# Two wide blocks a batch, near units of four blocks that may cross two batches, and softmax sums taken from a column of ones

## The chip, the cores and the metric

The kernel runs on one core of one Trainium2 chip. The metric is device microseconds of one execution; a kernel is judged by the median of several. A core has TensorE (PE in the profile; its weight loads are PEld), VectorE (DVE), ScalarE (ACT), GpSimd (POOL) and SyncE (SP, which here only issues DMAs). Every engine works through its own instructions in order and waits for others through semaphores.

## The reference

Block-sparse attention over 4 batches of 8 heads, 768 positions and 64 features, followed by a channel mix with a gate. Blocks are of 32 positions, 24 a batch.

```python
mask = np.abs(blk_i - blk_j) <= window            # window = 1
mask = mask | (blk_i == 0) | (blk_j == 0) | (blk_i == n_blocks - 1) | (blk_j == n_blocks - 1)
for qb in range(n_blocks):
    for kb in sampled_blocks[qb]:                 # three drawn blocks a row of blocks
        mask[qb * block:(qb + 1) * block, kb * block:(kb + 1) * block] = True
attn = softmax(where(mask, scale * q @ k.T, -1e9)) @ v
...
xk = mu_k * x + (1.0 - mu_k) * x_prev             # x is attn, heads side by side: 768 x 512
xr = mu_r * x + (1.0 - mu_r) * x_prev
k = np.maximum(xk @ w_k, 0.0)                     # 512 -> 1024
v = k * k @ w_v                                   # 1024 -> 512
out = sigmoid(xr @ w_r) * v
```

So query blocks 0 and 23 see every key, and each of the other 22 sees eight slots of 32 keys: the two end blocks, itself and its two neighbours, and three drawn blocks. A slot can repeat another one: a drawn block can be an end block, a neighbour or an earlier draw, and near the ends a neighbour is an end block. Such a repeat must count once.

## The kernel before

**Units.** A unit is four query blocks of one batch, 128 rows. Each batch has one wide unit, made of blocks 21, 22, 23 and 0 (`WIDE_BLOCKS`, line 32), and five near units of blocks 1 to 20. `UNITS` (line 202) starts with the wide units of batches 0, 1 and 2, then two near units of batch 0, then the wide unit of batch 3, then the other near units.

**A wide unit** (`wide_pair`, line 552) goes through four pairs of heads. For a pair, TensorE multiplies 128 query rows by 384 keys at a time (`sw`, line 563; two heads lie in the two halves of the contracted partitions), VectorE adds a mask and finds the extreme while it copies to `p` (`soft`, line 479), ScalarE takes exp and the sum with it (`exp`, line 489), TensorE transposes (`tw`, line 500), ScalarE copies the transposed tile (line 504), and TensorE multiplies by V, four blocks side by side in the array's columns (`o`, line 585). The keys lie in `k_ring`, which shares the memory tagged `k2` with the mixer's hidden values: the mixer's `k2` can't be taken before the last wide unit has let go of the ring.

**A near unit** is two groups of four heads (`near_group`, line 512). Each of the four blocks has its own tile of eight key slots (`KR`, five of them) and its own two tiles of V rows (`VR`, six): the three neighbours come by a plain load (line 468), the last block and the three drawn ones by a gather on POOL's queue (line 470). For a group there are 32 score matmuls in the profile (16 in the program, two passes each for f32) over 256 keys (`s`, line 524), then mask and extreme on VectorE, exp on ScalarE, two turns of four transposes (`t`, line 500) copied by VectorE (line 506), and 64 matmuls with V (`o`, line 546). Repeats are masked by -8e9 (`near_mask`).

**Finish** (line 593): reciprocal of the sums, the scaling, four transposes (`tx`, line 606) and the copy into `xt`, the transposed attention output of the batch. The wide units of batches 2 and 3 are finished long before their `xt` exists, so they go to a scratch tensor in HBM and come back later (`away`).

**The mixer** goes through three windows of 256 positions a batch, twelve in all. `split_x` (line 662) makes `xr` and `xk`, each as a pair of rounded high and low parts; every product is three matmuls. A window is two gates (`r`, line 713), four hidden pairs (`h`, line 731), squares on ScalarE and POOL, and two value products (`v`, line 760). Window 0 needs blocks 0 to 8 of its batch.

**Weights** arrive as float64 (10.5 MB) and are decoded by ScalarE, three VectorE operations (lines 365, 369, 373) and two POOL operations (lines 383, 387) for each of 20 tiles: 4 for `wr`, 8 for `wk`, 8 for `wv`.

**PSUM's eight banks**: two score tiles of two banks (`s`), one `o`, two for turns (`t`), one for the mixer (`m`).

**Order.** All operations are handed to a planner (`Plan`, line 83) with an estimated duration and a rank. `order` simulates the engines, picks among the operations that can start by rank, and so fixes the order in which each engine gets its instructions. The ranks come from tuned constants (line 844 and on); on the chip nothing but data waits and the order itself remain.

## Time and profile before

| what | value |
|---|---|
| median of 3 runs | 605.68 us (604.22 to 605.9) |
| profiled execution, span from first to last instruction | 616.1 us |
| PE busy in that span | 575.8 us (93%) |
| PEld, POOL, DVE, ACT busy | 465.5, 344.0, 303.8, 300.6 us |
| bytes moved by DMA | 114.18 MB, mean 185 GB/s |

The profiled execution has no time of its own beside its span; the span is 10.4 us (1.7%) longer than the median. Durations in the profile are of that execution, so a sum made of them stands against 616.1 us. Busy time of PE counts a matmul from its start to a modelled end, so some waiting inside a run of matmuls counts as busy.

### The profile page before, as it was taken

The page shows a single profiled execution, that of the slowest core. Times are in us where ns is not written, and L with a number is a line of the kernel's source. Part 1 is how long each engine was busy: PE and PEld are TensorE (multiplying, and loading weights), DVE is VectorE, ACT ScalarE, POOL GpSimd, SP SyncE. Part 2 cuts the span into 40 slices and gives each one's busy share as a digit, 9 for nine tenths or more (in the row PEclk, how much of TensorE's full clock was granted, in tenths as well). Part 3 has the DMA queues.
Part 4 walks back from the last instruction along what each step waited for, and adds up shares of the span by engine and source line. Part 5 has one row for each costly group of instructions (what it writes and reads, how often), then busy time and mean ns, then how long its engine had stood idle before and what let it go on. Part 6 is the DMA issues. An engine that isn't in the chain of part 4 may idle for free.

```text
span 616.1 us, 20666 instructions
## 1 busy us (share of the span) xinstructions
PE 575.8 (93%) x8172; PEld 465.5 (76%) x8172; DVE 303.8 (49%) x906; ACT 300.6 (49%) x712; POOL 344.0 (56%) x400
## 2 busy tenths in 40 slices
PE   8887878798899999999999989999999999999997
PEld 3564655587667878878788778778778788989897
DVE  6677768873864255264443452653632532423300
ACT  3675845583544545355535534635545454333341
POOL 1324344865777737657836835546467464664551
PEclk9999989999899999999999999999999999999999
DMA  8959659858786667766764774774666620000001
GB/s 310 399 157 379 231 168 335 282 164 286 219 261 217 188 193 212 210 181 202 227 200 164 232 227 146 233 229 147 224 188 182 201 75 1 36 18 18 17 18 35
DMA packets 88499, 114.18 MB, mean 185 GB/s; under 512 B 12626, under 2 KB 59219, under 8 KB 88403
## 3 DMA queue, kind: packets, MB, share of 16 engines
q1 hardware_dynamic: 81570, 91.79, 46.7%
q0 software_dynamic: 6400, 20.98, 10.7%
q8 instruction: 65, 1.06, 0.7%
q10 hardware_dynamic: 432, 0.10, 0.2%
q14 instruction: 32, 0.25, 0.1%
HBM read 106.01 MB, written 6.82 MB: 183 GB/s over the span
## 4 chain that ended last, share of the span: by engine, by line
PE 63%; DVE 10%; ACT 8%; issue 6%; POOL 5%; DMA 3%; another core or an unknown queue 2%; SPq 2%; ACTq 0%; DVEq 0%; POOLq 0%
PE v L760 17%; PE o L546 5%; PE h_1p L731 5%; PE h_3p L731 5%; PE r_0p L713 5%; PE t L500 5%; PE r_1p L713 4%; PE h_2p L731 4%; ACT p L489 4%; PE s L524 3%; PE h_0p L731 2%; PE tw L500 2%; PE sw L563 2%; PE o L585 2%
## 5 line engine op out<-in xcount | busy, mean ns | idle before, releaser
L760 PE MATMUL v<-wv,k 128*128 128x512 f32 (+1 forms) x600 | 139.4, 386 | 1.4 <-DVE z L768 1.4
L760 PEld LDWEIGHTS v<-wv,k 128*128 128x128 f32 x600 | 107.5, 188 | 26.5 <-DVE xr_2f L680 2.1
L489 ACT ACTIVATE p<-p,nm 128x256 f32<-128x256 f32 x160 | 79.4, 498 | 48.7 <-DVE nm L479 48.7
L470 POOL DMA_INDIRECT VR<-vt,lines x80 | 79.0, 988 | 33.1 <-PE o L546 16.0
L506 DVE COPY pt<-t 128x512 f32<-128x512 f32 x80 | 53.0, 686 | 81.5 <-PE t L500 74.6
L479 DVE CUSTOM_DVE_ANT_1 p<-s,near_mask 128x256 f32<-128x256 f32 x160 | 57.9, 418 | 30.4 <-remote 19.4
L689 POOL TENSOR_TENSOR xr<-xr_1f,xr 128x256 fp32r<-128x256 f32 x24 | 17.7, 740 | 72.0 <-ACT xr L687 71.9
L524 PE MATMUL s<-KR,q 64*32 64x256 f32 x1280 | 50.8, 381 | 1.0 <-PE tw L500 0.9
L500 PE MATMUL t<-ident,p 128*128 128x128 f32 x320 | 47.5, 283 | 3.8 <-ACT p L489 2.3
L546 PEld LDWEIGHTS o<-VR,pt 128*32 128x32 f32 x2560 | 37.9, 110 | 15.0 <-issue 8.8
L546 PE MATMUL o<-VR,pt 128*32 128x64 f32 x2560 | 44.7, 221 | 2.3 <-issue 1.4
L687 ACT CAST xr<-xr_1f 128x256 fp32r<-128x256 f32 x24 | 9.7, 405 | 72.9 <-PE r_0p L713 43.0
L731 PE MATMUL h_1p<-xk,wk 128*128 128x256 f32 x288 | 37.0, 283 | 8.2 <-ACT h_0k L744 4.6
L609 DVE TENSOR_TENSOR x<-o,R 128x512 f32<-128x512 f32 x24 | 16.6, 691 | 56.8 <-PE o L546 53.7
L500 PEld LDWEIGHTS t<-ident,p 128*128 128x128 f32 x320 | 36.9, 144 | 9.3 <-ACT p L489 6.4
L731 PEld LDWEIGHTS h_1p<-xk,wk 128*128 128x128 f32 x288 | 34.7, 188 | 10.3 <-ACT h_0k L744 5.5
L731 PEld LDWEIGHTS h_0p<-xk,wk 128*128 128x128 f32 x288 | 34.9, 188 | 3.6 <-issue 3.3
L713 PE MATMUL r_1p<-wr,xr 128*128 128x512 f32 x144 | 37.7, 411 | 0.0
L524 PEld LDWEIGHTS s<-KR,q 64*32 64x32 f32 x1280 | 27.1, 105 | 13.8 <-issue 3.8
L731 PE MATMUL h_3p<-xk,wk 128*128 128x256 f32 x288 | 36.8, 282 | 0.4 <-ACT h_2k L744 0.4
L731 PEld LDWEIGHTS h_2p<-xk,wk 128*128 128x128 f32 x288 | 34.6, 188 | 3.3 <-ACT k L745 3.3
L731 PE MATMUL h_0p<-xk,wk 128*128 128x256 f32 x288 | 36.9, 283 | 0.0
(115 smaller groups left out, 1043.7 us busy)
## 6 DMA issues: line engine op xcount, KB each, us to landing
VR<-vw SPq DMA_DIRECT2D x80, 256.0 KB
KR<-kd SPq DMA_DIRECT2D x80, 192.0 KB
KR<-kt SPq DMA_DIRECT2D x240, 64.0 KB
k_ring<-kq SPq DMA_DIRECT2D x16, 384.0 KB
VR<-vt SPq DMA_DIRECT2D x24, 256.0 KB
q<-qt SPq DMA_DIRECT2D x23, 256.0 KB
out<-z SPq DMA_DIRECT2D x23, 256.0 KB
early_w<-w_k SPq DMA_DIRECT2D x8, 512.0 KB
```

The lines of the kernel that those rows point to most:

```text
L470: plan.add(POOL, GATHER, at - LEAD_V + 0.01 * j, lambda w=w, n=n: nc.gpsimd.indirect_dma_start(VR[w].ap[:, 1, :], None, vt.rearrange("b n ...
L479: nc.vector.tensor_tensor_reduce(out=p.ap[:, cs].rearrange("p (a x) -> p a x", x=BLK), in0=view().rearrange("p (a x) -> p a x", x=BLK), in ...
L489: plan.add(ACT, 280 + 0.83 * (cs.stop - cs.start), rank, lambda: nc.scalar.activation(p.ap[:, cs], p.ap[:, cs], AF.Exp, bias=nm.ap[:, col ...
L500: nc.tensor.transpose(tp.ap[:, i, :], p.ap[:, cs], ident.ap)
L506: plan.add(DVE, 600, rank + 0.1, lambda: nc.vector.tensor_copy(out=pt.ap, in_=tp.ap), reads=[(tp,)], writes=[(pt,)])
L524: nc.tensor.matmul(s.ap[ROWS[j], row, a * 256 : (a + 1) * 256].rearrange("p (n x) -> p n x", x=BLK), q.ap[half, hp, ROWS[j]], KR[keys[j]]. ...
L546: nc.tensor.matmul(o.ap[ROWS[j], h * D : (h + 1) * D], pts[i // 2].ap[:, 2 * (i % 2) + g, ROWS[j]], VR[values[j]].ap[:, g, h * D : (h + 1) ...
L609: plan.add(DVE, 600, rank, lambda: nc.vector.tensor_tensor(out=x.ap.rearrange("p (h d) -> p h d", d=D), in0=o.ap.rearrange("p (h d) -> p h ...
L689: plan.add(POOL, 80 + 2.4 * MIX * tw, rank + O_MIX, lambda f=f, cs=cs: nc.gpsimd.tensor_tensor(out=dst.ap[:, 1, cs], in0=f.ap, in1=dst.ap[ ...
L713: nc.tensor.matmul(pr.ap[:, 0:512], xr.ap[:, a, c, :], wr.ap[:, w, c, :], start=(c == 0 and m == 0), stop=(c == CC - 1 and m == 2))
L731: nc.tensor.matmul(ph.ap[:, ff * TT : (ff + 1) * TT], wk.ap[:, w, c, f * P : (f + 1) * P], xk.ap[:, a, c, :], start=(c == 0 and m == 0), s ...
L760: nc.tensor.matmul(pv.ap[:, 0:width], k2.ap[:, a, f, i * P : (i + 1) * P], wv.ap[:, w, f, cs], start=(f == 0 and m == 0), stop=(f == FC - ...
```

## The change

**Units.** A wide unit is now two blocks, 0 and 23, which see all keys without a mask. The 22 near blocks of two batches make 44, that is eleven near units of exactly four blocks; the sixth is mixed (blocks 21 and 22 of the first batch, 1 and 2 of the second). In all there are 4 wide and 22 near units, ordered pair of batches by pair: wide, two near, wide, three near, mixed, five near. The scratch tensor in HBM is gone, and so is `k_ring`: wide keys lie in the same `KR` tiles as near keys, of which there are two, each for a whole unit.

**Wide.** With 64 query rows, two head pairs lie side by side in the array's columns: a score matmul is a 64x64 tile over 384 keys. VectorE finds the extremes of one score tile in one reduction. Half a unit (`wide_unit`, four heads) takes both score tiles.

**Near.** The keys of a unit are one run of six neighbouring blocks, two ends and twelve drawn blocks. A score matmul of 256 keys becomes one of 192 (three neighbours and three drawn) and one of 64 (the ends). There is no mask: repeats get V rows that are zero (row 3072 on of `vt`, through the gather's list), and V has a 65th column of ones, so the product with V gives the sum too, without the repeats. VectorE finds four extremes in one reduction over the 1024 scores; ScalarE takes exp straight from PSUM and no longer adds up. Turns are copied by ScalarE, except one in four from unit 6 on.

**Buffers.** Turns, finishes and mixer share two PSUM banks tagged `m`; `o` has two. `dif` goes from two buffers to one, `pt` from four to three. For unit 1 the drawn keys are loaded from ScalarE's queue.

**Planner.** It gets larger durations, a limit of eight DMAs in flight, and a model of PE's instruction supply (`code`, `feed`); release times and ranks are now lists, one for each unit, window and weight tile.

```diff
+QB = 4
+NEARS = NB - 2
+
+
+def near_units(pair):
+    b, c = 2 * pair, 2 * pair + 1
+    units = [[(b, n + j) for j in range(QB)] for n in range(1, NB - QB, QB)]
+    mixed = [(b, NB - 3), (b, NB - 2), (c, 1), (c, 2)]
+    return units, mixed, [[(c, n + j) for j in range(QB)] for n in range(3, NB - 1, QB)]
+
+
+ENDS, DRAWN = 2 * QB, 2 * QB + 2
+KEYS = DRAWN + QB * NRAND
+DV = D + 1
+HD = H * DV
...
-UNITS = [(0, 0), (1, 0), (2, 0), (0, 1), (0, 2), (3, 0)]
-UNITS += [(b, u) for b in range(B) for u in range(1, NC + 1) if (b, u) not in UNITS]
-
-AWAY = 2
...
+def all_units():
+
+    units = []
+    for pair in range(B // 2):
+        first, mixed, second = near_units(pair)
+        wide = [[(b, 0), (b, NB - 1)] for b in (2 * pair, 2 * pair + 1)]
+        units += [wide[0], *first[:LATER[pair]], wide[1], *first[LATER[pair]:], mixed, *second]
+    return units
...
+            twice, keep, line = (e.ap[:, :, SEEN + i : SEEN + i + 1] for i in range(3))
+            v.tensor_tensor(out=same, in0=first.to_broadcast([P, NEARS, SEEN]), in1=c[:, 0:stat].rearrange("p (a b) -> p a b", b=SEEN), op=ALU.is_equal)
+            v.tensor_reduce(out=twice, in_=same, axis=AX.X, op=ALU.max)
+            v.tensor_tensor(out=same[:, :, 0 : NRAND - 1], in0=first.to_broadcast([P, NEARS, NRAND - 1]), in1=r.ap[:, :, 1:], op=ALU.is_equal)
+            for i in range(NRAND - 1):
+                v.tensor_tensor(out=twice, in0=twice, in1=same[:, :, i : i + 1], op=ALU.max)
+            v.tensor_scalar(out=twice, in0=twice, scalar1=c[:, stat + 2 : stat + 3], scalar2=None, op0=ALU.mult)
+            v.tensor_scalar(out=keep, in0=twice, scalar1=-1.0, scalar2=1.0, op0=ALU.mult, op1=ALU.add)
+            v.tensor_scalar(out=line, in0=first, scalar1=c[:, stat : stat + 1], scalar2=c[:, stat + 1 : stat + 2], op0=ALU.mult, op1=ALU.add)
+            v.tensor_tensor(out=line, in0=line, in1=keep, op=ALU.mult)
+            v.scalar_tensor_tensor(out=line, in0=twice, scalar=float(B * S), in1=line, op0=ALU.mult, op1=ALU.add)
+            for b in range(B):
+                v.scalar_tensor_tensor(out=lines.ap[:, b, :].unsqueeze(2), in0=keep, scalar=float(b * S), in1=line, op0=ALU.mult, op1=ALU.add)
...
+    def near_keys(r):
+        return KR[r].ap.rearrange("p (n x) -> p n x", n=KEYS)
+
+    def wide_keys(r, a):
+        return KR[r].ap[:, a * S : (a + 1) * S]
...
+                due = at + SECOND[2 + (b > 0)] * k - LEAD_W
+                for a in range(2):
+                    plan.add(SP, ISSUE, due, lambda r=r, a=a, hp=k + 2 * a: nc.sync.dma_start(wide_keys(r, a), kq[b, hp]),
+                             writes=[(KR[r], *WIDE_PARTS[a])], release=due, size=393216)
...
+        if mixed:
+            slots[r] = None
+            c = members[-1][0]
+            near(0, b, 0, 1)
+            near(NB - QB, b, 1, QB)
+            near(0, c, QB + 1, QB)
+            near(NB - 1, c, 2 * QB + 1, 1)
+            where = [(1 + j, 0, QB) for j in range(2)] + [(QB + 1 + j, QB + 1, 2 * QB + 1) for j in range(2)]
+        else:
+            near(n0 - 1, b, 0, QB + 2)
+            if slots[r] != b:
+                slots[r] = b
+                plan.add(SP, ISSUE, at_k, lambda: nc.sync.dma_start(
+                    near_keys(r)[:, ENDS:DRAWN], kt[b * NB : (b + 1) * NB : NB - 1].rearrange("n p x -> p n x")),
+                    writes=[(KR[r], ENDS, ENDS + 1)], release=at_k, size=65536 * 2)
+            where = [(j, ENDS, ENDS + 1) for j in range(QB)]
+        issuer, by = (ACT, nc.scalar) if i in KEYS_BY_ACT else (SP, nc.sync)
...
+        tp = buf([P, 4, P], F32, "m", M_BUFS, f"t{name}", ps)
+        pt = buf([P, 4, P], F32, "pt", PT_BUFS, f"pt{name}")
...
+    def direct_exp(p, out, s, view, nm, rank, key):
+        width = out.stop - out.start
+        plan.add(ACT, 210 + 0.835 * width, rank, lambda: nc.scalar.activation(
+            p.ap[:, out], view(), AF.Exp, bias=nm(), scale=SCALE), reads=[(s,), key[0]], writes=[(p, key[1])], table="exp")
...
+            s = buf([P, 2, 512], F32, "s", 2, f"s{name}", ps)
+            nm = buf([P, 4], F32, "base", 2, f"nm{name}")
+            p = buf([P, 4 * 256], F32, "p", P_BUFS, f"p{name}")
+
+            def mm(s=s, gi=gi):
+                K = near_keys(r)
+                for a in range(2):
+                    hp = 2 * gi + a
+                    xs = slice(hp * BLK, (hp + 1) * BLK)
+                    for part in range(2):
+                        for j, (near, e0, e1) in enumerate(where):
+                            for row, half in enumerate(HALF):
+                                to = s.ap[ROWS[j], row, a * 256 : (a + 1) * 256].rearrange("p (n x) -> p n x", x=BLK)
+                                if part:
+                                    to, k = to[:, 3:5], K[half, e0 : e1 + 1 : e1 - e0, xs]
+                                else:
+                                    drawn = DRAWN + NRAND * j
+                                    k = K[half, near : near + 3, xs]
+                                    k = bass.AP(tensor=k.tensor, offset=k.offset, ap=[k.ap[0], [(drawn - near) * HP * BLK, 2], *k.ap[1:]])
+                                    to = bass.AP(tensor=to.tensor, offset=to.offset, ap=[to.ap[0], [5 * BLK, 2], [BLK, 3], [1, BLK]])
+                                nc.tensor.matmul(to, q.ap[half, (hp * QB + j) * BLK : (hp * QB + j + 1) * BLK], k,
+                                                 start=True, stop=True, skip_group_check=True)
...
+            def top(s=s, nm=nm):
+                nc.vector.tensor_reduce(out=nm.ap.rearrange("p (r a) -> p r a", r=2),
+                                        in_=s.ap.rearrange("p r (a x) -> p r a x", a=2), axis=AX.X, op=ALU.max)
+                nc.vector.tensor_scalar(out=nm.ap, in0=nm.ap, scalar1=-SCALE, scalar2=None, op0=ALU.mult)
...
+            pts = [turn([(p, x * P) for x in range(4 * k, 4 * k + 4)], f"{name}_{k}", t1 + O_TR[kind], DVE if at >= TURN_FROM and (gi, k) in TURN_DVE else ACT) for k in range(2)]
...
+            def pv(pts=pts, gi=gi):
+                for row in range(2):
+                    for a in range(2):
+                        i, h = 2 * a + row, 4 * gi + 2 * a + row
+                        for g in range(2):
+                            for j in range(QB):
+                                nc.tensor.matmul(
+                                    o[gi].ap[ROWS[j], i * DV : (i + 1) * DV], pts[row].ap[:, 2 * a + g, ROWS[j]],
+                                    VR[values[j]].ap[:, g, h * DV : (h + 1) * DV], start=(g == 0), stop=(g == 1), skip_group_check=True)
...
+                def mm(s=s, k=k, i=i):
                     for row, half in enumerate(HALF):
...
+                        for a in range(2):
+                            hp = i + 2 * a
+                            nc.tensor.matmul(
+                                s.ap[HALF[a], row, 0:W], q.ap[half, 2 * hp * BLK : 2 * (hp + 1) * BLK],
+                                wide_keys(keys[i], a)[half, k * W : (k + 1) * W], start=True, stop=True, skip_group_check=True)
+
+                plan.add(PE, N_WIDE_S, t1, mm, reads=[(q,), (KR[keys[i]], *range(KEYS))], writes=[(s,)], table="wide", code=16)
+                plan.add(DVE, 930, t1 + O_MAX[kind], lambda s=s, k=k, nm=nm: nc.vector.tensor_reduce(
+                    out=nm.ap[:, k, :], in_=s.ap[:, :, 0:W], axis=AX.X, op=ALU.max), reads=[(s,)], writes=[(nm, k)])
...
+            def recip(i=i, each=each):
+                r = R.ap[:, each, :]
+                nc.vector.tensor_scalar(out=r, in0=o[i].ap.rearrange("p (h d) -> p h d", d=DV)[:, :, D:DV], scalar1=1e-9, scalar2=None, op0=ALU.add)
+                nc.vector.reciprocal(r, r)
...
-                d = buf([P, tw], F32, "dif", 2, f"{name}d{c}")
+                d = buf([P, tw], F32, "dif", 1, f"{name}d{c}")
...
-            tags = [("m", M_BUFS), ("t", T_BUFS), ("o", 1), ("s", 2), ("s", 2)]
+            tags = [("m", M_BUFS), ("o", 2), ("s", 2), ("s", 2)]
...
-KR_BUFS, VR_BUFS, P_BUFS, PT_BUFS, T_BUFS, M_BUFS = 5, 6, 4, 4, 2, 1
-
-T_ACT = ((0, 1, 2), (0, 1, 2))
...
+KEYS_BY_ACT = [1]
+FIRST_NEAR = 1
+TURN_DVE = frozenset([(1, 1)])
+TURN_FROM = 6
+LATER = (2, 2)
...
+    picks = drawn[np.arange(1, NB - 1)[None, :, None], turns[np.arange(P) // BLK][:, None, :]]
...
+    vb = np.concatenate([vb, np.ones_like(vb[..., :1])], axis=4).reshape(B, NB, BLK, HD)
+    vt = np.concatenate([vb.reshape(B * S, HD), np.zeros((BLK, HD), v.dtype)])
+    vb = np.concatenate([vb, np.zeros((B, 1, BLK, HD), v.dtype)], axis=1)
```

More of the change, by code (lines that the diff above doesn't have):

```diff
@@ L79 @@
 class Op:
-    __slots__ = ("engine", "ns", "lag", "fn", "rank", "deps", "users", "bufs", "end", "start", "table", "seq", "waits", "release", "size")
+    __slots__ = ("engine", "ns", "lag", "fn", "rank", "deps", "users", "bufs", "end", "start", "table", "seq", "waits", "release", "size", "code", "dmas")
 class Plan:
@@ L132, in add, with feed @@
         return op
+    CHUNK, FIRST, FETCHED, FLIGHT = 257, 204, 4600, 8
+    def feed(self, op, at, ns):
+        end, left, since = at, op.code, self.crossed
+        upto = self.upto
+        while left >= upto:
+            end += ns * upto / op.code
+            end = since = max(end, since + self.FETCHED)
+            left -= upto
+            upto = self.CHUNK
+        return end + ns * left / max(op.code, 1), since, upto - left
     def order(self):
         free, table, avail = {}, {}, {}
-        queue_free = 0.0
+        self.crossed, self.upto = 0.0, self.FIRST
+        queue_free, lands = 0.0, [0.0] * self.FLIGHT
         for op in self.ops:
@@ L149, in order @@
                     at = max(now, op.release)
+                    if op.size and engine != "POOL":
+                        at = max(at, lands[-self.FLIGHT])
                     for d in op.deps:
@@ L217, in block_sparse_attention_channel_mix @@
     ctx: ExitStack, tc: tile.TileContext,
-    kt, kd, kq, qt, vt, vw, blocks, rows, picks, consts, mu_k, mu_r, w_k, w_v, w_r, out, wide,
+    kt, kd, kq, qt, vt, vw, blocks, picks, consts, mu_k, mu_r, w_k, w_v, w_r, out, wide,
 ):
@@ L427, in load_unit @@
+    def load_unit(i, members, at):
+        q = buf([P, HP * P], F32, "q", 2, f"q{i}")
+        lead = i == 0
+        due = -60 if lead else at - LEAD_Q
+        many = len(members)
+        b, n0 = members[0]
+        plan.add(SP, ISSUE, due, lambda: nc.sync.dma_start(q.ap[:, 0 : HP * many * BLK], qt[i, :, 0 : HP * many * BLK]),
+                 writes=[(q,)], release=at - LEAD_Q, size=65536 * many)
         keys, values = [], []
-        if u == 0:
-            for hp in range(HP):
-                r = Part(k_ring, K_RING)
+        if not n0:
+            for k in range(2):
+                r = place(0)
@@ L436, in load_unit @@
+            for k in range(NB // QB // 2):
                 w = place(1)
@@ L664, in split_x @@
         blocks = range(max(t0 - 1, 0) // BLK, (t0 + tw - 1) // BLK + 1)
[L665 removed]
+        ready = sorted({unit_of[b, n] for n in blocks}) + ["z"]
         x = xt[b]
```

550 lines of the change are left out of this document (228 added, 322 removed).

## The prediction

> **What bounds the kernel now.** I read the page's head first, then busy time by stage.
>
> ```profile
> span 616.1 us, 20666 instructions
> PE 575.8 (93%) x8172; PEld 465.5 (76%) x8172; DVE 303.8 (49%) x906; ACT 300.6 (49%) x712; POOL 344.0 (56%) x400
> ...
> 0.00:70.00 70.00, 58.42 (x1196) 37.56 (x1196) 48.66 (x152) 43.46 (x86) 23.08 (x35) 1.00 0.88 314
> 70.00:131.00 61.00, 49.60 (x1104) 34.31 (x1101) 47.63 (x127) 35.63 (x89) 32.08 (x38) 0.97 0.70 221
> 131.00:157.00 26.00, 22.84 (x420) 19.86 (x420) 14.31 (x41) 14.26 (x41) 16.83 (x17) 0.99 0.85 269
> 157.00:523.70 366.70, 355.79 (x4911) 293.79 (x4912) 169.92 (x526) 177.98 (x445) 225.77 (x266) 1.00 0.62 190
> 523.70:616.10 92.40, 89.19 (x552) 79.95 (x551) 23.32 (x64) 29.28 (x53) 46.22 (x46) 1.00 0.07 24
> ```
>
> The columns are the stretch, its length, then PE, PEld, DVE, ACT, POOL, the granted clock, DMA share and GB/s. PE sets the end: from 157 us on it is never free for long, while no other engine is busy for more than 62% of a long stage. Only before 157 us is it short of work. There DMA runs at a share of 0.7 to 0.88 and DVE at 70 to 78%.
>
> Busy time hides waits inside runs of matmuls, so I take the dense price of each piece from the chain of waits, where PE is never idle inside a piece.
>
> ```profile
> 14.48 0.59 PE tw L500 x4
> ...
> 23.25 1.02 PE tw L500 x8
> ...
> 36.75 0.59 PE tx L606 x4
> ...
> 64.57 1.48 PE o L585 x96
> 66.05 1.49 PE sw L563 x8
> ...
> 270.49 1.02 PE t L500 x8
> ...
> 373.24 1.02 PE s L524 x32
> ...
> 377.29 1.03 PE o L546 x64
> ...
> 523.67 2.81 PE r_0p L713 x12
> ...
> 534.78 2.83 PE h_1p L731 x24
> ...
> 556.97 2.80 PE r_0p L713 x12
> ...
> 584.77 2.80 PE r_0p L713 x12
> ...
> 601.68 11.22 PE v L760 x72
> ```
>
> A mixer window alone takes 584.77 - 556.97 = 27.8 us; twelve take 333.6. A near unit before is 2 x (1.02 s + 1.02 t + 1.03 o) + 0.59 tx = 6.73; twenty take 134.6. A wide unit before is 4 x (1.49 sw + 1.53 tw + 1.48 o) + 0.59 = 18.6, with 1.53 as one and a half times 1.02; four take 74.4. The warming matmuls take 7.3. Together 549.9 us, so 66.2 of the 616.1 are lost.
>
> Where are they lost? The last matmul ends at 601.68 + 11.22 = 612.9: 3.2 at the end. For the middle stage I count its near matmuls with V.
>
> ```profile
> 157.00:523.70 366.70, 37.57 (x2176) 31.98 (x2176) 1.00 0.62 190
> ```
>
> 2176 at 128 a unit are 17 near units, 114.4 us. The mixer does 89.2 after 523.7 (612.9 - 523.7) and one gate and four hidden pairs, 14.1, before 157, so 230.3 in between. 344.7 dense in 366.7: 22.0 lost, 6.4%. What is left, 41.0, is lost before 157.
>
> ```profile
> 81.30 1.27 POOL L387 TENSOR_TENSOR wk<-wf,wk 128x512 fp32r<-128x512 f32 x1
> ...
> 111.78 3.05 PE L713 MATMUL r_0p<-wr,xr 128*128 128x512 f32 x12
> ...
> 130.97 1.55 PE L585 MATMUL o<-VR,ptw 128*32 128x64 f32 x96
> 132.45 3.10 PE L731 MATMUL h_0p<-xk,wk 128*128 128x256 f32 x24
> ```
>
> These rows of the timelines say why. The last tile of `wk` is ready at 82.6, the first gate starts at 111.8, and the first hidden pair at 132.45, right behind the last product of batch 3's wide unit, whose key ring holds the memory of `k2`. Until the mixer starts, PE has attention alone, and attention alone can't fill it: a near unit loads 24 key blocks of 64 KB, eight V tiles of 256 KB and q, 3.9 MB by the code, which is 14 us at the 271 GB/s that the first 131 us average (70 at 314, 61 at 221), against 6.7 us on PE.
>
> **The change, part by part.**
>
> *Wide units.* With 64 rows and two head pairs side by side, `sw` has as many matmuls a unit as before (32) of as many keys. `s` at L524 shows that small tiles run beside each other: 32 matmuls of 256 keys in 1.02 us is 32 ns each, where two row halves alone (L563) give 186 ns for 384. So four quadrants halve the time: 2.98 us. If the columns didn't overlap it would be 5.96. Transposes fall from 48 to 24, 3.06; products with V from 384 to 192 at 15.4 ns, 2.96; tx 0.30. A unit takes 9.3 instead of 18.6: **-37.2** for four.
>
> *Near units.* There are 22 instead of 20. The score matmul is split, so a group has 64 where it had 32. By columns, the 192-key half costs 32 x 24 ns and the 64-key half 32 x 8 (columns alone) to 32 x 16 ns (what an `o` matmul of 64 columns takes, 1.03 / 64). That is 1.02 to 1.28; I take the middle, 1.15. A 65th column on 64 adds under 0.02 to a group and is left out. A unit is 2 x (1.15 + 1.02 + 1.03) + 0.59 = 6.99, 22 are 153.8: **+19.2**.
>
> The Trainium skill speaks against this split: "TensorEngine Tiling (Array Packing)", Instruction Overhead, says that a matmul costs about 60 cycles however small. By that page's 60 cycles as an unshared price, 25 ns at the 2.4 GHz that the Trainium skill gives for TensorE ("Trainium Kernel Development and Optimization", NeuronCore Architecture; the product is an estimate), a group would gain 0.8 us, not 0.13; the `o` row, 16 ns for a whole matmul, disagrees, since neighbours overlap. What it would do as a rule of this kernel is rival C.
>
> Dense work after: 549.9 - 37.2 + 19.2 = **531.9**.
>
> *VectorE and ScalarE.*
>
> ```profile
> L479 DVE CUSTOM_DVE_ANT_1 p<-s,near_mask 128x256 f32<-128x256 f32 x160 | 57.9, 418 | 30.4 <-remote 19.4
> L506 DVE COPY pt<-t 128x512 f32<-128x512 f32 x80 | 53.0, 686 | 81.5 <-PE t L500 74.6
> ...
> L489 ACT ACTIVATE p<-p,nm 128x256 f32<-128x256 f32 x160 | 79.4, 498 | 48.7 <-DVE nm L479 48.7
> L489 ACT ACTIVATION_READ_ACCUMULATOR p<-p,nm 128x1 f32 x160 | 29.9, 187 | 0.0
> L504 ACT COPY ptw<-tw 128x512 f32<-128x512 f32 x48 | 26.7, 586 | 11.5 <-PE tw L500 11.2
> ```
>
> The separate reading of sums disappears (29.9 us of ACT), about 70 of the 88 near turns move from DVE to ACT (70 x 0.59 = 41 us), and four masked passes become one reduction of 1024 scores, no dearer than the four (1.7). Neither engine was near its limit after 157 us (46 and 49%), so this gives nothing by itself there; the cover is the mixer's matmuls, and without it each turn would show its 0.59. In the first stage DVE was at 70%, and there it helps. The list of gathers moves from POOL to DVE and replaces the two mask functions: some fifteen small operations for some twenty, nothing. The single `dif` buffer and three `pt` lie under `split_x`, which works a step ahead of its gate.
>
> *The start.* Window 0 now needs only units 0, 1 and 2 and the twelve tiles of `wr` and `wk`; the ring is gone. These bring 3.2 + 7.1 + 6.3 MB = 16.6 (a near unit now has 18 key blocks), which at the first stage's 314 GB/s is 53 us. On DVE, the three wide units and twelve tiles took until 82.6; a two-block wide unit, two near units and twelve tiles are about 48 us of work at the same 70%, 68 us. I put the first dense hidden pair at 70 us. PE has then done 7.3 + 9.3 + 14.0 and about half of the second wide unit, 35 us: **35 lost** instead of 41 by 157. Ends: 25 (start at 55) and 47 (start at 90, which the 82.6 of the tiles would give). The twelve key loads on ScalarE's queue, waiting in front of the first exp for the list of drawn blocks, are inside these ends.
>
> *The middle.* The dense work left is 531.9 - 35 - 89.2 = 407.7; at 6.4% it loses 26.1. The mixer's second bank takes away one wait.
>
> ```profile
> L731 PE MATMUL h_1p<-xk,wk 128*128 128x256 f32 x288 | 37.0, 283 | 8.2 <-ACT h_0k L744 4.6 <-ACT p L489 2.6 <-issue 1.0
> ```
>
> The 4.6 us behind `h_0k` is the bank still being copied. What is late next is a turn that wants the same two banks; I keep its price for rival B. **21.5 lost**, between 11 (half) and 40 (with two thirds of rival D on top).
>
> Sum: 531.9 + 35 + 21.5 + 3.2 = **591.6** against 616.1. The span is 1.017 times the median, so 591.6 x 605.68 / 616.1 = 581.6, **582 us**.
>
> **The rivals.**
>
> *A, the mixer doesn't start early (slower).* If tiles or `xt` come late, PE goes on with attention at the DMA's pace. By 131 us, at those 271 GB/s, 35.5 MB have come, less 10.5 of weights: two wide units and five near, 61 us of PE work, 69 lost. The sum is 625.6, **615 us**. Between (70, 35) and (131, 69) the loss grows 0.56 us for each us; it decides from a start at about 114. For it: the tiles took until 82.6 although eight had room in the buffer early. Against it: the ring, the reason for 132, is gone.
>
> *B, two banks for turns, finishes and mixer (slower).* 88 + 24 + 26 uses of a bank, each held through a 0.59 copy on ACT. PE waiting out half of each adds 40 us: 631.6, **621 us**; it decides from 0.18 us a use. Against: a 2.83 us hidden pair fits beside each copy.
>
> *C, a score matmul costs per instruction, not per column (slower).* At 32 ns each, `s` takes 2.04 a group, 44 x 0.89 = 39 more: 630.8, **620 us**. Against: the 16 ns of `o`.
>
> *D, PE's instruction supply (no change).*
>
> ```profile
> 22.27 0.98 PE L585 MATMUL o<-VR,ptw 128*32 128x64 f32 x53 [0.56 <-issue]
> 23.18 1.09 PE L500 MATMUL tw<-ident,pw 128*128 128x128 f32 x8
> 24.20 0.92 PE L563 MATMUL sw<-k_ring,q 64*128 64x384 f32 x4
> 25.05 1.09 PE L585 MATMUL o<-VR,ptw 128*32 128x64 f32 x62
> 28.57 0.72 PE L585 MATMUL o<-VR,ptw 128*32 128x64 f32 x34 [2.42 <-issue]
> ```
>
> Between the two stalls lie 127 matmuls with their loads, 254 instructions, in 6.3 us: a supply of about 256 each 6.3. A near group goes from 208 instructions to 272, 6.7 us of supply for 3.2 of work. With only one hidden pair beside it (48 more) it has 7.9 of supply for 6.1: 1.8 lost. A third of the groups so, 15, is 27 us: 618.6, **608 us**. Against: after 157 us a group has 7.6 us of mixer beside it.
>
> *E, better.* `s` at 1.02, start at 55, half the middle's loss: 526.2 + 25 + 11 + 3.2 = 565.4, **556 us**.
>
> **Chances.** Forecast (570 to 600) 0.64, E 0.12, D 0.08, A 0.08, B 0.04, C 0.04. The range of 562 to 606 leaves out most of E and A to C. What can be told from no change here is 0.3%, 1.8 us. Faster is the forecast, E and half of D, 0.80; same 0.04; slower 0.16.
>
> **What would show it.** The first hidden pair at 55 to 90 us, and PE's dense pieces: `s` near 1.15 with 64 matmuls, a wide unit's `sw` with 8 matmuls in 0.75. PE's idle time after the start stays under 25 us, with no large group behind ACT's copies (B) or "issue" (D). The forecast is wrong if the first hidden pair starts after 114 us, or if PE waits for copies of `t` by tens of microseconds.

## The result and the profile after

The changed kernel takes 632.85 us (median of 4 runs, 630.44 to 634.34) beside 605.47 us for the kernel before on the same chip: a ratio of 1.045, with a 95% interval of 1.042 to 1.048. The forecast was 582 us, so it was wrong in sign and by 51 us.

The page's head and chain of the kernel after, whose profiled execution took 631.75 us:

```profile
span 630.0 us, 22052 instructions
PE 567.6 (90%) x9132; PEld 477.5 (76%) x9132; DVE 289.6 (46%) x580; ACT 300.1 (48%) x590; POOL 357.2 (57%) x402
...
PE 67%; DMA 10%; DVE 9%; issue 5%; POOL 4%; ACT 3%; SPq 1%; ACTq 0%; POOLq 0%; DVEq 0%
```

PE is busy for 8 us less than in the profile before, but the span is longer: PE stands still more often. A new profile of the unchanged kernel (run `before_again`, 605.8 us) had a span of 604.1, so the 616.1 on which the prediction stood isn't usual where this kernel takes 605 us. On three other chips, where it takes about 619 us, spans of 615.4 to 621.1 are usual, and the first profile's 4.6 us wait behind `h_0k`, which the second lacks, is there again in two runs of its variants (`b_near` 4.9, `b_wide` 5.3). So whether that first profile was one long execution or came from such a chip stays open. From here on the kernel before means the second profile. Busy time by stage, first of the kernel before, with the columns that the prediction explained:

```profile
0.00:100.00 100.00, 83.44 (x1715) 54.85 (x1716) 68.90 (x214) 58.77 (x130) 34.28 (x48) 0.95 0.79 278
100.00:200.00 100.00, 91.24 (x1631) 73.16 (x1630) 73.27 (x180) 57.34 (x144) 73.97 (x84) 0.98 0.77 251
200.00:500.00 300.00, 299.03 (x4164) 249.44 (x4164) 141.02 (x444) 151.56 (x379) 185.49 (x216) 1.00 0.64 197
```

and of the kernel after:

```profile
0.00:100.00 100.00, 60.52 (x1214) 39.41 (x1215) 67.69 (x118) 40.40 (x82) 51.61 (x59) 0.82 0.83 276
100.00:200.00 100.00, 92.61 (x1821) 79.56 (x1822) 48.62 (x96) 54.70 (x112) 72.75 (x81) 0.97 0.75 239
200.00:500.00 300.00, 288.39 (x4814) 246.17 (x4796) 125.42 (x271) 152.57 (x300) 167.38 (x197) 0.98 0.57 180
```

Two stages differ. In the first 100 us both kernels move the same bytes (278 and 276 GB/s), but PE is busy for 83.4 us before and 60.5 after. From 200 to 500 us PE before is busy for 299.0 of 300 us; after, for 288.4.

In the next table each kind of matmul has its median price in undisturbed runs, taken from the matmul records of both kernels; the rest of each stretch is called lost:

| term | predicted | measured |
|---|---|---|
| dense TensorE work | -18.0 | -16.3 |
| lost in the first stage (predicted until 157 us; measured until 200 us, 40.7 before and 68.0 after) | -6 | +27.3 |
| lost afterwards (measured 5.7 before and 21.3 after) | -0.5 | +15.6 |
| sum | -24.5 | +26.6 (spans: +25.9) |

The dense term was right; the rest was lost, in waits and in matmuls that took longer than their clean price. What PE waits for in the start shows in the chain of waits of the kernel after (start, length, what):

```profile
32.98 5.68 DMA KR<-kt
38.68 3.30 DMA KR<-kt
42.64 3.93 DMA KR<-kt
...
62.72 0.98 POOL VR L498
64.01 6.65 DMA VR<-vt,lines
...
80.21 2.39 DVE wmag L363
...
87.09 1.46 DVE xk_0f L722
```

13 us for the drawn keys of the first near unit, which ScalarE issues at 32 to 43 us, then a gather of V, then weight decoding and mixing on DVE until the first hidden pair at 99.4. In the kernel before, 38 of the first 100 us of the chain are PE's own `sw`, `tw` and `o` of wide units.

The longest of PE's waits in the first 100 us (us in total, times, longest), of the kernel after and below of the kernel before:

```profile
PE tx L664 <- DVE x L657: 8.1, 4, 3.9
PE sw L606 <- DMA q<-qt: 7.8, 1, 7.8
PE o L636 <- ACT ptw L519: 4.3, 2, 3.1
PE tw L515 <- ACT ptw L519: 4.0, 3, 3.1
PE sw L606 <- ACT pw L531: 3.5, 1, 3.5
PE o L583 <- issue: 2.8, 1, 2.8
```

```profile
PE o L585 <- issue: 3.2, 2, 2.4
PE tx L606 <- DVE x L609: 2.6, 2, 2.2
PE tw L500 <- ACT pw L489: 2.5, 2, 2.2
```

Summed over all rows of these views, PE waits 16.1 us behind ScalarE (3.8 before), 11.3 behind loads (none before), 8.1 behind VectorE (3.4) and 3.0 for "issue" (7.2), that is, for nothing that the profile shows. So what grew in the start is waiting for other engines and for loads. By the same prices as in the table, 54 of the first 100 us are lost after and 26 before.

The later loss has another look. These are the longest of PE's waits between 200 and 520 us, of the kernel after, and below all of them of the kernel before:

```profile
PE o L583 <- issue: 4.2, 4, 2.2
PE h_0p L773 <- issue: 2.3, 1, 2.3
PE t L515 <- ACT z L762: 2.0, 1, 2.0
PE r_1p L755 <- issue: 1.5, 1, 1.5
PE s L560 <- issue: 0.7, 1, 0.7
```

```profile
PE t L500 <- ACT p L489: 0.7, 2, 0.4
PE h_3p L731 <- ACT h_2k L744: 0.2, 1, 0.2
```

"Issue" is 8.7 us here after, none before. Over the whole kernel PE's waits are 58.5 us after, 14.5 of them "issue", and 26.0 before, 8.4 of them "issue". A timeline of the kernel after shows one such stop in the middle of a group of 64 products, where no semaphore stands:

```profile
400.28 0.54 PE L583 MATMUL o<-VR,pt 128*32 128x65 f32 x23
402.98 1.31 PE L583 MATMUL o<-VR,pt 128*32 128x65 f32 x40 [2.15 <-issue]
```

Of the 10 stops over 0.3 us inside runs of matmuls of one line after 150 us, 8 (11.1 us) fall on the same place (193 or 194) of every 256 TensorE instructions, counted over the whole trace; the kernel before has one such stop after 150 us, at another place. The page's line of the queue that brings instructions (packets, MB, share) has the same step:

```profile
q8 instruction: 72, 1.18, 0.8%
```

72 packets of 256 make 18,432, beside the 18,416 matmul, weight-load and wait records on TensorE (65 packets and 16,589 records in the kernel before). That is how the prediction's rival D, the instruction supply, would look. The Trainium skill, "Runtime: NRT & Kernel Launch", Instruction fetch mechanics, says that each engine's instructions are refilled in blocks of 256, and that the cost of a crossing is mostly hidden; the place of these stops agrees with the first, their 0.5 to 2.4 us not with the second.

### The profile page after: what moved, and what is told of

The parts are those of the page before. It is cut to its first block, busy times and chain, and to the rows that moved or that the text cites. A ratio compares the mean times of both kernels' runs of the same rounds, so it can differ in the third digit from the quotient of the medians.

```text
span 630.0 us, 22052 instructions
## 1 busy us (share of the span) xinstructions
PE 567.6 (90%) x9132; PEld 477.5 (76%) x9132; DVE 289.6 (46%) x580; ACT 300.1 (48%) x590; POOL 357.2 (57%) x402
## 4 chain that ended last, share of the span: by engine, by line
PE 67%; DMA 10%; DVE 9%; issue 5%; POOL 4%; ACT 3%; SPq 1%; ACTq 0%; POOLq 0%; DVEq 0%
PE v L802 18%; PE s L560 6%; PE o L583 6%; PE h_3p L773 5%; PE t L515 5%; PE r_0p L755 5%; PE h_2p L773 5%; PE h_0p L773 4%; PE r_1p L755 4%; PE h_1p L773 4%; DMA VR<-vt,lines 3%; DMA KR<-kt 3%; PE sw L606 2%; DMA q<-qt 2%; DVE nm L566 2%
## 5 line engine op out<-in xcount | busy, mean ns | idle before, releaser
L802 PE MATMUL v<-wv,k 128*128 128x512 f32 (+1 forms) x600 | 149.1, 395 | 0.5 <-issue 0.5
L531 ACT ACTIVATE p<-s,nm 128x256 f32<-128x256 f32 x176 | 71.5, 480 | 53.3 <-DVE nm L568 36.1
L566 DVE TENSOR_REDUCE nm<-s 128x4 f32<-128x1024 f32 x44 | 53.7, 1221 | 63.2 <-PE s L560 59.5
L583 PE MATMUL o<-VR,pt 128*32 128x65 f32 x2816 | 53.2, 223 | 11.9 <-issue 9.4
L560 PE MATMUL s<-KR,q 64*32 64x192 f32 (+1 forms) x2816 | 57.3, 281 | 4.2 <-DMA KR<-kt 3.5
L560 PEld LDWEIGHTS s<-KR,q 64*32 64x32 f32 x2816 | 49.0, 108 | 13.7 <-issue 11.0
L519 ACT COPY pt<-t 128x512 f32<-128x512 f32 x70 | 40.7, 589 | 32.7 <-PE t L515 30.9
L722 DVE SCALAR_TENSOR_TENSOR xr_1f<-xr_1d,mk,xt 128x128 f32<-128x128 f32 x48 | 19.0, 396 | 47.6 <-POOL xr L731 33.9
L810 DVE SCALAR_TENSOR_TENSOR z<-v,z 128x512 f32<-128x512 f32 (+1 forms) x25 | 16.7, 667 | 46.9 <-PE v L802 46.2
L773 PE MATMUL h_2p<-xk,wk 128*128 128x256 f32 x288 | 37.7, 285 | 0.0
```

The lines of the kernel that those rows point to most:

```text
L519: plan.add(ACT, 200 + 0.75 * P * many, rank + 0.1, lambda: nc.scalar.copy(pt.ap[:, 0:many], tp.ap[:, 0:many]), reads=[(tp,)], writes=[(pt,)])
L531: plan.add(ACT, 210 + 0.835 * width, rank, lambda: nc.scalar.activation(p.ap[:, out], view(), AF.Exp, bias=nm(), scale=SCALE), reads=[(s,) ...
L560: nc.tensor.matmul(to, q.ap[half, (hp * QB + j) * BLK : (hp * QB + j + 1) * BLK], k, start=True, stop=True, skip_group_check=True)
L566: nc.vector.tensor_reduce(out=nm.ap.rearrange("p (r a) -> p r a", r=2), in_=s.ap.rearrange("p r (a x) -> p r a x", a=2), axis=AX.X, op=ALU ...
L583: nc.tensor.matmul(o[gi].ap[ROWS[j], i * DV : (i + 1) * DV], pts[row].ap[:, 2 * a + g, ROWS[j]], VR[values[j]].ap[:, g, h * DV : (h + 1) * ...
L722: nc.vector.scalar_tensor_tensor(out=f.ap[:, i, :], in0=d.ap, scalar=mk.ap[:, which, c : c + 1], in1=x.ap[:, c, t0 : t0 + tw], op0=ALU.mul ...
```

## The experiments

The kernel before took about 605 us on one chip, 619 on three others and 624 on a fifth, so runs are compared by their ratio to the kernel before on the same chip. The changed kernel's own ratio is 1.045 on the first and 1.0395 (1.0357 to 1.0433) on one of the 619 us chips.

### Four causes for the late start

`before_again` is the kernel before as it is; it took 605.09 us.

> The kernel before, unchanged, for a second profile of it. The first profile had a span of 616.1 us against a median of 605.5. If that execution was merely a long one, this span is about 603 to 605; if the profile always adds 10 us to this kernel, it is again about 616.

`e_first` moves small loads and the finding of lists to the front of their queues:

```diff
-    for op in plan.order():
+    ops = plan.order()
+    for op in front + [o for o in ops if o not in front]:   # q of unit 0, number, con, pick, pack, find
         op.fn()
```

> The changed kernel with the query tile of unit 0, the list of drawn blocks, the constants and the two small VectorE functions that make the lists moved to the front of their queues; the rest in the same order. Theory A (attention starts late because small loads stand behind weights: first score matmul at 16.0 us, gather lists at 30.9, drawn keys of unit 1 landing at 46.6): 12 to 20 us faster, first score matmul at about 9. Theory B (VectorE, busy 98 and 92% in 60 to 100 us, sets the start of the mixer): under 3 us faster. Theory C (the granted clock, 0.73 to 0.84 in the first 60 us): about 5 faster, since TensorE waits less.

Measured: 1.049 (1.0426 to 1.0553). The first `sw` came at 7.26 us instead of 15.99, but the second stayed at 22.6 and unit 1's scores at 47. The extreme of the first scores, which the second `sw` needs by way of the exp, now stands at 18.3 us behind VectorE's decoding of a weight tile that landed at 12.0. So the theory that small loads alone make the start late falls.

`e_decode` lets two of the three decode operations of each weight tile work on 8 of 512 columns, so most of the decoding is left out:

```diff
-                m = mag.ap.bitcast(I32)
+                m = mag.ap.bitcast(I32)[:, 0:8]
```

> The changed kernel with two of the three VectorE operations of each weight tile done on 8 of 512 columns, so most of the decoding is left out; same order. Theory B: 12 to 25 us faster (some 15 tiles before 100 us, about 1.35 us less each), first hidden pair at about 80 instead of 99. Theory A and C: at most 4 us.

Measured: 1.042 (1.0393 to 1.0448), first hidden pair at 97.7 instead of 99.4. DVE ends the chain there, but leaving out most of its decoding gains two microseconds at most.

`e_warm` issues 44 warming matmuls instead of 20, since the granted clock is 0.82 in the first 100 us against 0.95 before:

> The changed kernel with 44 warming matmuls instead of 20, which fill TensorE until about 16 us; same order otherwise. Theory C: granted clock 1.0 at 16 us, the first 16 score matmuls in 1.5 instead of 2.8 us, 3 to 8 us faster. Theories A and B: within 2 us.

Measured: 1.055 (1.049 to 1.061). The first group of 16 `sw` matmuls still took 2.84 us, and the granted clock over the first 100 us was 0.78. More warming doesn't cure the low clock, and costs time.

### Loads and cover

`e_double` does the TensorE work of the first two wide units twice (+18.3 us), `e_halfw` loads only half of each tile of `w_r` and `w_k` (3.1 MB less; the other half is zero), `e_stores` puts each output store 12 us later in SP's order.

> The changed kernel with the matmuls of the first two wide units (scores, transposes, products with V) done twice, results the same, order the same: 18.3 us more of TensorE work in the first 100 us. Theory D (the start is set by the loads, 27 MB at about 280 GB/s, and TensorE's work there is hidden under them, so that the wide work which the change saved was worth nothing): at most 5 us slower. If TensorE's work sets the start: 18 us slower.

> The changed kernel with the twelve tiles of w_r and w_k loaded by half (the other half is zeros from twelve small memsets on POOL, 0.6 us each), so half of these weights is left out: 3.1 MB less in the first 60 us, same order. Theory D: 8 to 12 us faster, first hidden pair near 90 instead of 99. If not the bytes but the order of the engines sets the start: within 3 us.

> The changed kernel with each store of the output put 12 us later in SyncE's order, so that loads behind it do not stand behind a store whose data is not there (97 us of waiting on SyncE's queue in the profile); rest in the same order. Theory E (after 200 us TensorE waits for loads that are issued late in SyncE's queue): 5 to 12 us faster. If the lateness comes from the buffers or from POOL's queue: within 3 us.

Measured: 1.0566 (1.0503 to 1.063), 1.0378 (1.0333 to 1.0424) and 1.039 (1.0348 to 1.0433). Against 1.0395 to 1.045 the first is 7 to 11 us more, so some half of the added work was hidden; the other two are 0 to 5 us less, which can't be told from nothing. 3.1 MB at the 276 GB/s of the first 100 us would be 11 us, and the first hidden pair of `e_halfw` came at 101.3 us, no earlier: the start isn't set by the bytes alone. No run moves the drawn keys of unit 1 off ScalarE's queue or changes ScalarE's copies, so these two rivals stand untested.

`e_gathers`, with every gather 5 us earlier in POOL's order, came out at 759.2 us. This order changes what the kernel computes, so it tells nothing about the theory. How, the trace doesn't show: the first gather, at 30.9 us, still waits for the operation that makes its list.

> The changed kernel with each gather of V rows put 5 us earlier in POOL's order. Theory F (after 200 us TensorE waits for gathers that stand behind the mixer's work on POOL; three waits of 5 to 7 us in the chain): 5 to 10 us faster. If POOL then only waits for the buffers at the gather, and the mixer's work stands behind it: no gain, or a few us slower.

Next came a theory on the order. The planner that writes the order prices a load at 370 GB/s with 0.67 us behind it. A replay of the written order with 300 GB/s and 2.0 us put its end at 632 us; for the kernel before, the same prices give 588. So the new order might be laid out too tight. Three kernels tested that: `l_after` and `l_before` halve every plain load of keys and values (64 of 128 partitions; the gathers of V stay whole) after the first use of a buffer, and `e_order` has the order written again with 300 GB/s, 2.0 us and 5.4 us per 257 TensorE instructions, and the constants searched anew.

```diff
-    RING, RING_POOL, RATE, DONE = 650, 1000, 370, 670
+    RING, RING_POOL, RATE, DONE = 650, 1000, 300, 2000
```

> The changed kernel once more, as the base of this group. Every theory expects its ratio again, 1.04 to 1.05, with a first hidden pair near 99 us.

> The changed kernel with every load of keys and values cut to half its bytes (64 of 128 partitions) from the second use of a buffer on; the rest of the buffer keeps what it held, so half of the keys and values are left out of the result. Instructions, order and waits are the same. Theory L (the loads set the pace: the order is laid out against 370 GB/s, and the chip serves loads as if at about 300 GB/s with 2 us of delay): replaying the written order with those prices gives 632 us, and 599 us with these loads halved, so L expects 33 us less, about 600 us. Rival R (TensorE's side sets the pace: instruction supply, stalls inside its own order, banks): under 10 us less, 623 us or more.

> The kernel before with the same cut of its loads of keys and values. Theory L: the same replay gives 587.6 us, and 583.6 with the loads halved, so 4 us less (up to 8 at 290 GB/s), about 599 to 601 us: then the two kernels with light loads stand level or the changed one is ahead, and what the change loses is in the loads. Rival R: also little change here, and the changed kernel still 3 to 4% behind it.

> The changed kernel with the same loads, computing and buffers, but with its order written anew: the planner's prices of a load set to 300 GB/s and 2.0 us, that of 257 TensorE instructions to 5.4 us, and the constants searched again under those prices. Theory L: the replay puts the end at 610 us where it put the old order's at 632, so 20 us less, about 612 us, ratio 1.01: most of the loss was in the order, and the rest (some 7 us over the kernel before) in loads that bring less TensorE work per byte. Rival S (the loss is in the structure: the bytes before the first mixer pair cannot come sooner, whatever the order): 3 us less or none, ratio 1.04.

Measured: `after_again` 1.0395, `l_after` 1.0495 (1.0452 to 1.0537), `l_before` 1.0228 (1.0186 to 1.0269), `e_order` 1.034 (1.0283 to 1.0397). All three miss theory L. Halving the loads made both kernels slower. One reason may be that the issue itself became dearer. The rows are SP's issues of the V tiles (min, median, max in ns), of `after_again` and of `l_after`:

```profile
L496 SPq DMA_DIRECT2D VR<-vw x88: 3/382/2365, 17.8 to 543.8; - x88
```

```profile
L507 SPq DMA_DIRECT2D VR<-vw x88: 3/547/2127, 17.7 to 559.9; - x88
```

So this pair doesn't isolate bytes. The new order took 638.9 us beside 642.6 for `after_again` on the same chip, 3.7 less with overlapping intervals, where the replay promised 20, and in its chain another engine stands where loads stood:

```profile
PE 67%; POOL 9%; issue 7%; DMA 5%; DVE 5%; ACT 3%; SPq 2%; ACTq 0%; POOLq 0%; DVEq 0%
```

A replay fitted to one order didn't carry over to the next. By `e_order`, theory L falls as the main cause; that the bytes have no part isn't shown.

### The parts of the change, one at a time in the kernel before

`b_wide` leaves out five sixths of the value matmuls of the wide units (-19.7 us of TensorE work), `b_near` does half of the near units' score matmuls twice (+20 us, about what the change adds), `b_split` and `b_parts` split each score matmul in two over six and two key blocks.

```diff
-                for n, i in enumerate(mine):              # b_wide; start and stop follow
+                for n, i in enumerate(mine[:1]):
...
-            for a in range(2):                            # b_near
+            for a in (0, 1, 0):
...
+                for part in (slice(0, 6), slice(6, 8)):   # b_parts: outside j; b_split: inside j
```

> The kernel before with five sixths of the value matmuls of its wide units left out (one key chunk of six is summed, so the wide rows are incomplete); loads, order and all else are the same. This takes some 19.7 us of TensorE work out of the wide units. Theory W (the wide units' TensorE work lies under loads in the kernel before, so that saving it gains little): 0 to 8 us faster, ratio 0.987 to 1.0. Rival V (it is paid in full, as the prediction had it): 16 to 20 us faster, ratio 0.967 to 0.974.

> The kernel before with half of the score matmuls of each near group done a second time (same result): 0.51 us more a group, 20 us more TensorE work in 40 groups, about what the change adds to its near units (19.2 us), and 1,280 more TensorE instructions. Theory N (work added to near units is paid in full, since they share the mixer's stage): 17 to 25 us slower, ratio 1.028 to 1.041. If loads hide it too: under 10 us, ratio below 1.017. W and N together would give the change its loss: what it saves is hidden, what it adds is paid.

> The kernel before, with each score matmul of a near group split in two, over six and two key blocks, as the changed kernel has it (64 matmuls a group instead of 32; same result). The groups' own time rises by 0.13 to 0.17 us each, 5 to 7 us in all. Theory D: 2,560 more TensorE instructions also bring gaps of supply, 12 to 18 us slower in all, ratio 1.02 to 1.03. Theory L: only the 5 to 7 us, of which the units of the first 200 us hide a part: ratio 1.005 to 1.011.

> The kernel before, with each score matmul split in two as before over six and two key blocks, but all the long ones of a head pair first and then the short ones, in the order that the changed kernel has (same result). In the changed kernel such a group of 64 takes 1.19 us against 1.02 us for 32, so the groups' own time rises by 0.17 us each, 6.8 us in 40. If that is all: ratio 1.009 to 1.013. Theory D (the supply of 2,560 more TensorE instructions costs on top, 8 to 11 us in the changed kernel): ratio 1.022 to 1.032. If it comes out near 1.048, as with the short and the long ones alternating, the number of matmuls matters and not their order.

`b_wide`: 0.9833 (0.9797 to 0.9869), 10.3 us less, so 52% of the saved work arrived, between both theories. `b_near`: 1.031 (1.0278 to 1.0342), 19.2 us more: work added to near units is paid in full (a clean group took 1.46 us instead of 1.02, so the added work is 17.6 us and not 20). `b_split`: 1.0478 (1.0417 to 1.0539), far above both expectations. `b_parts`: 1.0453 (1.0403 to 1.0504), so by its expectation it's the number of matmuls that matters and not their order. Splitting the score matmuls, with the same loads, the same result and no other part of the change, costs the kernel before as much as the whole change does.

Where does it go? A clean group of 64 takes 1.19 us in `b_parts` against 1.02 for 32, 6.8 us in 40 groups. The rest is stops. From a group's first score matmul to the next other matmul, the 40 groups take 81.7 us in all, where clean ones would take 47.6; in the kernel before it is 49.1 and 40.8. These are the page's rows of matmuls (PE) and of weight loads (PEld), with busy time, mean ns, idle time in front of them and what ended most of it, first of the kernel before, then of `b_parts`. One stop can stand in both rows, so they aren't to be added:

```profile
L524 PE MATMUL s<-KR,q 64*32 64x256 f32 x1280 | 51.3, 391 | 0.9 <-PE tw L500 0.9
L524 PEld LDWEIGHTS s<-KR,q 64*32 64x32 f32 x1280 | 27.1, 108 | 13.8 <-issue 4.0
```

```profile
L525 PE MATMUL s<-KR,q 64*32 64x64 f32 (+1 forms) x2560 | 64.9, 276 | 18.8 <-issue 17.5
L525 PEld LDWEIGHTS s<-KR,q 64*32 64x32 f32 x2560 | 47.2, 105 | 35.2 <-issue 32.1
```

A timeline of `b_parts` shows one such group:

```profile
240.81 0.91 PE L547 MATMUL o<-VR,pt 128*32 128x64 f32 x52
241.65 1.68 PE L525 MATMUL s<-KR,q 64*32 64x192 f32 x50
243.62 0.29 PE L525 MATMUL s<-KR,q 64*32 64x64 f32 x2 [0.29 <-issue]
244.38 0.28 PE L525 MATMUL s<-KR,q 64*32 64x64 f32 x3 [0.47 <-issue]
245.10 0.37 PE L525 MATMUL s<-KR,q 64*32 64x64 f32 x9 [0.44 <-issue]
245.40 3.00 PE L732 MATMUL h_0p<-xk,wk 128*128 128x256 f32 x14
```

A group of products (64 matmuls and 64 weight loads) runs straight into a group of scores. After some 228 instructions in 2.4 us TensorE gets only 4 to 8 more in each 0.7 us, with all key tiles long in use. Such a group comes once in two near units and takes 3.7 us; before, with 192 instructions in that place, it took 1.6. Groups behind four transposes stay at 1.19, but for two at 2.0. Where `b_parts` has 1,280 matmuls more, `b_near` has 640, of 32 ns each: between 200 and 520 us PE's "issue" is 9.6 us in the first and 0.7 in the second.

The stop has a second price. From 245.9 to 249.3 us the trace's clock record stands at a half, and the hidden pair behind the group takes 4.46 us. That happens in 7 of the 12 windows of `b_parts` (4.4 to 4.5 us instead of 2.8 to 2.9, with the clock at 0.62 or 0.63 in the mean), 10.7 us in all. In `b_split` no hidden pair `h_0p` is longer than 2.94.

The same rows for the kernel after, scores and then products:

```profile
L560 PE MATMUL s<-KR,q 64*32 64x192 f32 (+1 forms) x2816 | 57.3, 281 | 4.2 <-DMA KR<-kt 3.5
L560 PEld LDWEIGHTS s<-KR,q 64*32 64x32 f32 x2816 | 49.0, 108 | 13.7 <-issue 11.0
L583 PE MATMUL o<-VR,pt 128*32 128x65 f32 x2816 | 53.2, 223 | 11.9 <-issue 9.4
L583 PEld LDWEIGHTS o<-VR,pt 128*32 128x32 f32 x2816 | 43.9, 110 | 23.7 <-issue 17.4
```

In front of these matmuls PE's "issue" is 10 us, against 3.5 before. By the measure of whole groups, scores and products of near units lose 32 us in the kernel after and 13 before; some 6 of the 32 are waits for loads. In the kernel after the scores stay mostly clean (12 us lost in 44 groups, 34 in the 40 of `b_parts`) and the products lose 20. The planner after the change has a price for the supply (4.6 us for 257 instructions), and in its order one run of scores starts right behind products, where `b_parts` has 12. So the split isn't paid in the changed kernel in the place where `b_parts` pays it, and only a part of the changed kernel's loss is of this kind.

`e_ends` goes the other way: in the changed kernel one matmul of 128 query rows takes the two end keys for four blocks, 40 matmuls a group instead of 64.

```diff
-                                to, k = to[:, 3:5], K[half, e0 : e1 + 1 : e1 - e0, xs]
...
+                            nc.tensor.matmul(to[:, 3:5], q.ap[half, (hp * QB + j) * BLK : (hp * QB + j + same) * BLK],
+                                             K[half, e0 : e1 + 1 : e1 - e0, xs], start=True, stop=True, skip_group_check=True)
```

> The changed kernel, same order, with the scores against the two end keys taken for four blocks (two, in the mixed units) in one matmul instead of four: the result is the same, and a group of scores issues 40 matmuls instead of 64, 1.0 to 1.1 thousand matmuls fewer in all. Theory D (TensorE's instruction supply: in the changed kernel the gaps inside runs of matmuls after 150 us stand at the same place of every 256 TensorE instructions, some 13 us in all, and hardly any in the kernel before): 8 to 12 us less, ratio 1.02 to 1.03. Theory L (loads pace it): 0 to 3 us less, ratio 1.035 to 1.045.

Measured: 1.0503 (1.0471 to 1.0534), slower by some 3 to 7 us than the changed kernel's ratios, against both theories. The wider matmuls seem not to run beside the narrow ones; their weight loads wait in front of them, without any gap in the matmul rows themselves:

```profile
L563 PEld LDWEIGHTS s<-KR,q 64*128 64x128 f32 (+1 forms) x384 | 26.7, 181 | 28.3 <-issue 28.3
L563 PE MATMUL s<-KR,q 64*128 64x64 f32 (+1 forms) x384 | 39.2, 293 | 0.1
```

A clean group went from 1.19 to 1.71 us, 23 us in 44 groups. The stops inside runs of one line at the place 193 or 194 of 256 fell from 13.0 us (`after_again`) to 2.4, so fewer instructions did take those away, but the new form cost more than they had.

## Why the prediction was wrong

- *Dense work (531.9, or -18).* Right: measured -16.3. A score group took 1.19 us where 1.15 was predicted, eight `sw` matmuls some 0.8 where 0.75 was, hidden pairs and gates were unchanged. Rival C, a price per score matmul, is out: 64 take 1.19 us, 19 ns each.
- *The wide units' -37.2.* The size was right, the counting of it was not. The step subtracted it from a sum to which all waiting was added by a rate. In the kernel before, the wide units are what PE does while keys, V and weights arrive. `b_wide` shows 52% of such a saving arriving at the end (41 to 64% by its interval), `e_double` shows about half of added work hidden. If one half holds for the whole 37.2, some 18 us of it were never there to be had. These are not on top of the start's loss below; they are a part of it, seen from the other side.
- *The near units' +19.2.* Right, and paid in full (`b_near`: 19.2 us for 17.6 of added work).
- *"35 lost", with the first hidden pair at 70 us.* This step failed most: the first stage was to lose 6 us less and lost 27 more, 33 of the 51 us by which the forecast was off. The pair came at 99.4, and 54 us were lost in the first 100. The prediction's own line through (70, 35) and (131, 69) gives 51 at 99, so the relation held and the time was wrong (the 69 should be 70 by its own terms, 131 less 61). The time was made from bytes over GB/s and DVE's busy share, while the chain shows a sequence of waits, for drawn keys, a gather and the decode, and PE's own waits behind ScalarE grew from 3.8 to 16.1 us in the first 100. None of the single causes tried (small loads, decode, clock, weight bytes) took more than 5 us off the time, so which of these waits sets the start stays open.
- *"21.5 lost" in the middle.* As a change this failed too, with -0.5 predicted and +15.6 measured. In size it came near, 18 us lost after 200 us without the 3.2 at the end, but by luck: the 22.0 it was made from are losses of the first profile, its waits behind ScalarE among them, and the second has next to none. So the wait behind `h_0k`, for which 4.6 us were taken off, wasn't there to be removed on this chip; on a 619 us chip the second bank may have removed it (`after_again` has none). Rival B's waits for copies are small after 200 us (the 2.0 us behind `z` is the largest of them); in the start PE does wait for ScalarE's copies, which B didn't price by stage. And something like rival D, given 0.08 and a price of 27 us, happened: PE's stops without a shown cause went from 0 to 8.7 us between 200 and 520 us, and over the whole kernel, in front of scores and products, from 3.5 to 10. Its argument against, that each group has mixer beside it, looked at the average spacing; in `b_parts` the slow groups are those that follow products directly.
- *The scale 605.68 / 616.1.* It belonged to one profile that the second didn't repeat; by the second, span and time are 1.7 us apart. As a difference, -24.5 us of span, the forecast hardly depends on it. As a sum it does: the span came out 38 us above 591.6 (33 in the start, 9 in dense prices, 3 less afterwards), and the other 13 of the 51 come from taking 10 off for the scale.

What is shown: the split of the score matmuls alone costs the kernel before 4.5%, and work added to near units is paid in full while about half of what is saved in wide units isn't returned. What is only argued: that the stops are TensorE's instruction supply. The profile names no releaser. The even place in every 256 instructions of the changed kernel, the dependence on the burst and the stops of `e_ends` fit; but in `b_parts` only 2 of 27 stops over 0.3 us after 150 us stand at that place, so its stops may not be the same thing. What stays open is what makes the start late. PE's "issue" waits fell there, so such stops aren't it; the waits that grew are for loads, ScalarE and VectorE, and no single cause tried there moves them. No version here beats the kernel before.

## What to carry to other kernels

Before counting a saving in busy time, ask what the engine would do in its place: in a stage that waits for loads, half of it was gone. Count instructions as well as columns when a matmul is split, and look at the longest burst of small ones and not at the average, for the price shows as idle time that the profile calls "issue". Count such idle time once: rows of matmuls and of their weight loads can show the same stop. And when an order is written by a planner, a change of the work changes the order too, so test a part of the change alone in the old kernel: here one part cost as much there as the whole change does, though the changed kernel pays in other places.

## What the runs showed of the hardware

- After some 228 TensorE instructions in 2.4 us, further ones came at 4 to 8 in each 0.7 us (`b_parts`, from 241 us on), and the granted clock then stood at a half for 3.4 us.
- A load of a V tile to 64 partitions with half the bytes took SP a median of 547 ns to issue, against 382 ns for 128 partitions, in both kernels.
- Score matmuls of 32 query rows run eight side by side (19 ns each); with matmuls of 128 rows of the array's columns among them, a group of the same columns took 1.71 us instead of 1.19 (`e_ends`). Alternating lengths cost too: 1.37 us in `b_split`, where long and short ones alternate, 1.19 in `b_parts`.
- The granted clock fell to 0.82 over the first 100 us where PE was short of work (0.95 in the kernel before); 24 more warming matmuls didn't help (0.78).
